# Window attention and a highway layer on one core: the steps of five engines laid out in one order table

## The chip, the cores and the metric

The kernel runs on one core of a Trainium2 chip. The core has a matrix engine (TensorE, PE in the profile, with its weight loads as PEld), VectorE (DVE), ScalarE (ACT), GpSimd (POOL) and a queue for transfers (SyncE, SP), each with its own queue of instructions. The metric is the device time of the core in microseconds (us), from the launch's first to its last instruction; lower is better.

## The reference

Attention over 4 batches, 8 heads, 768 positions of 64 elements. A query sees the first 4 positions (the sink) and the 128 positions up to its own (the window). The result, as 3072 tokens of 512 elements, goes through a highway layer.

```python
keep = is_sink | ((rel >= 0) & (rel < 128))      # rel = query position - key position
a = softmax(where(keep, q @ k.T / 8, -1e9))
x = (a @ v).reshape(3072, 512)
H = maximum(x @ w_h, 0)
T = 1 / (1 + exp(-(x @ w_t + b_t)))
out = T * H + (1 - T) * x
```

## The kernel before

The work is cut into NB = 24 blocks of 128 queries, 6 per batch. Keys and values of block n are a chunk of 128 rows shifted by 64, so a block's queries need their own chunk whole ("A" parts, 128 columns of EW = 192) and half of the chunk on either side ("B" parts, 64 columns). Block n therefore needs q of n and k and v of n-1, n and n+1.

A block goes through these steps. pe_T (L222) transposes q or k by head pairs on TensorE into the second half of a score tile's PSUM banks, and act_T (L232) copies the transpose out to SBUF as qT or kT, on ScalarE, or on VectorE where an engine is given. pe_SA and pe_SB (L266, L275) make the scores, four heads in each of two groups g; act_S (L288) takes the exponential of one group on ScalarE, into e; dve_mask (L295) multiplies it by the window's mask on VectorE. pe_sink (L249) makes the sink scores of one block, or of two blocks at a time after the first batch, and act_sink (L258) their exponential, es. pe_AB and pe_AA (L304, L317) sum the values, with a column of 2.0 beside each head's values that gives the softmax's denominator. dve_rec and dve_x (L334, L339) divide: x, in the program xh. pe_X (L346) transposes x, act_X (L353) copies the transpose to SBUF as xT. pe_Mt and pe_Mh (L358, L372) multiply by w_t (after a bias row) and by w_h; act_u (L367) takes a tanh of the first; dve_d, dve_e and dve_o (L380, L386, L392) form max(h, 0) - x, times (1 + u), plus 2x, and the output's transfer starts. The factors of 2 take the place of the sigmoid, and undo each other.

Order is written by hand. Under manual_schedule every engine runs its instructions in the order in which the program calls the steps, so a wait of one instruction holds all that its engine has behind it. Semaphores for the data between engines are added for it.

PSUM is what couples the steps. The pool ps_s has two score tiles, one per group; a transpose of q or k lies in such a tile as well, either in a tile that a block's scores use next (it is then "hosted" by that block), or in a tile of its own ("lone"). A tile is free again when the exponential and the copy have read it. The pool ps_m has two banks, which sink scores, xtp, tps and hps take in turn in the order of the program: the third of them waits until the first has been read. ps_av holds the values of one block.

Loads run ahead by AHEAD = 8 blocks, all issued by GpSimd, one instruction for each of q, k and v. In the start GpSimd issues q0, k0, k1, v0, v1, q1 and k2, then makes the four triangles of the mask, then goes on with w_h and later loads. VectorE's more_constants (L184) clears buffers, waits for the mask, makes two variants of it (mask0, mask1) and scales the bias (bt16).

Blocks 0 to 3 are written out one call after another: the scores of a block come group by group (lone_S, scores and exponential of group 0 and then of group 1), and transposes are lone, q on ScalarE and k on VectorE. From block 3 on a loop over i runs the steps of several blocks: the scores of n = i + 1, the masks of group 1 of i, xT of i - 1 on VectorE, d and e of i - 2, the values of i, the sink scores of n, o of i - 2, the gate and h of i - 1, the transpose of x of i. So h is one block behind the values, and d, e and o two. From n = TS = 5 on block n hosts the transposes of q and k of n + 2.

Of the kernel before, what the change touches and what calls it, by code (L numbers as in the profile page):

```python
# [20 lines left out]
def kernel(  # L21
# [106 lines left out]
    with tc.manual_schedule(engines={ENG.DVE}):  # L128
        nc.vector.memset(k_first[0:HP], 0.0)
        nc.vector.memset(v_ring[0][0:HP, 0:H * 65], 0.0)  # L130
        nc.vector.memset(warm, 0.0)
        nc.vector.memset(ident, 1.0)
        nc.vector.memset(ebias, _EXP_BIAS)
        nc.vector.memset(mask, 1.0)
        nc.vector.memset(bm, 1.0)
        for vt in v_ring:
            init_v(vt)

    def tri(t, rows, lo, hi, base, step, cm):
        nc.gpsimd.affine_select(  # L140
# [11 lines left out]
    with tc.manual_schedule(engines={ENG.Pool, ENG.SP}):  # L152
        nc.sync.dma_start(out=bt32, in_=moe_b_t.unsqueeze(0))
        for b in range(B):
            nc.sync.dma_start(out=vs_dn[b], in_=v[b, :, 0:NSINK, :])
        load_q(0)
        load_k(0)
        load_k(1)
        nc.gpsimd.affine_select(
            out=ident, in_=ident, compare_op=ALU.is_equal, fill=0.0,  # L160
            base=0, pattern=[[-1, P]], channel_multiplier=1)
        load_v(0)
        load_v(1)
        load_q(1)
        load_k(2)
        tri(mask, slice(0, HP), 0, P, HP - 1, -1, 1)
        tri(mask, slice(HP, P), 0, P, 0, 1, -1)
        tri(mask, slice(0, HP), P, EW, 0, 1, -1)
        tri(mask, slice(HP, P), P, EW, -1, -1, 1)
        load_w(moe_w_h, wh_sb)  # L170
        nc.gpsimd.affine_select(
            out=bm, in_=bm, compare_op=ALU.is_ge, fill=0.0,
            base=0, pattern=[[-NSINK, H]], channel_multiplier=1)
        nc.gpsimd.affine_select(
            out=bm, in_=bm, compare_op=ALU.is_ge, fill=0.0,
            base=NSINK - 1, pattern=[[NSINK, H]], channel_multiplier=-1)
        load_v(2)
        load_q(2)
        load_k(3)
        load_w(moe_w_t, wt_sb)  # L180
        load_v(3)


    def more_constants():  # L184
        nc.vector.memset(bt16, 0.0)
        nc.vector.memset(ones_row, 0.0)
        nc.vector.memset(ones_row[0:1, :], 1.0)
        for i in range(2):
            nc.vector.memset(ks_bd[i], 0.0)
            nc.vector.memset(vs_bd[i], 0.0)  # L190
            nc.vector.memset(es_t[i], 0.0)
        nc.vector.tensor_copy(out=mask0, in_=mask)
        nc.vector.memset(mask0[0:HP, 0:P], 0.0)
        nc.vector.memset(mask0[HP:HP + NSINK, 0:P], 1.0)
        nc.vector.memset(mask0[HP:P, P:EW], 0.0)
        nc.vector.tensor_copy(out=mask1, in_=mask)
        nc.vector.memset(mask1[HP:HP + NSINK, P:EW], 0.0)
        nc.vector.tensor_scalar_mul(bt16[0:1, :], bt32, 0.5)

    def sink_ones():  # L200
        for i in range(2):
            nc.vector.tensor_scalar_mul(vs_bd[i][0:NS4, :, D:D + 1],
                                        bm[0:NS4, :].unsqueeze(2), 2.0)
# [110 lines left out]
                    rhs=vt[src, 65 * h:65 * h + _AVN], start=(h % 4 == 0), stop=False,  # L314
                    skip_group_check=True)

    def pe_AA(n):  # L317
        av = av_of[n]
        vt = v_ring[n % NV]
        b, c = divmod(n, NSC)  # L320
        for h in range(H):
            nc.tensor.matmul(  # L322
                av[:, h // 4, h % 4, 0:_AVN], lhsT=e_at(n, h)[:, 0:P],
                rhs=vt[:, 65 * h:65 * h + _AVN], start=False,
                stop=False, skip_group_check=True)
        if c:
            for g in range(2):
                nc.tensor.matmul(
                    av[:, g, :, 0:65], lhsT=es_of[n],
                    rhs=vs_bd[b % 2][:, 4 * g:4 * g + 4, :], start=False, stop=True,  # L330
                    skip_group_check=True)
        av_of[n] = av.rearrange("p g h e -> p (g h) e")
# [65 lines left out]
    def on(n):  # L398
        return 0 <= n < NB

    def has_sink(n):
        return 0 < n < NSC or on(n) and n % 2 == 1

    def load_set(n):
        if on(n):
            load_q(n)
            load_k(n + 1)
            load_v(n + 1)

    def lone_T(nq, nk):  # L410
        if nq is not None:
            pe_T(("q", nq), 0, q_sd.pop(nq))
            act_T(("q", nq), 0, qT, nq)
        if nk is not None:
            pe_T(("k", nk), 1, k_sd.pop(nk))
            act_T(("k", nk), 1, kT, nk, nc.vector.tensor_copy)

    def lone_S(n):
        for g in range(2):
            pe_SA(n, g)  # L420
            pe_SB(n, g)
            act_S(n, g)

    TS = 5

    with tc.manual_schedule(engines={ENG.PE, ENG.DVE, ENG.Activation, ENG.SP, ENG.Pool}):
        warm_up(8)
        more_constants()
        for n in range(3, AHEAD):
            load_set(n)  # L430
        pe_T("q0", 0, q_sd.pop(0))
        act_T("q0", 0, qT, 0)
        pe_T("k0", 1, k_sd.pop(0))
        act_T("k0", 1, kT, 0, nc.vector.tensor_copy)
        pe_T("k1", 0, k_sd.pop(1))
        act_T("k1", 0, kT, 1)
        lone_S(0)
        dve_mask(0, 0)
        dve_mask(0, 1)
        lone_T(1, 2)  # L440
        sink_ones()
        sink_v(0, nc.vector)
        fill_ks(0, nc.vector)
        pe_AB(0)
        pe_AA(0)
        dve_rec(0)
        dve_x(0)
        lone_S(1)
        pe_sink(1)
        act_sink(1)  # L450
        dve_mask(1, 0)
        dve_mask(1, 1)
        pe_X(0)
        act_X(0)
        pe_AB(1)
        pe_AA(1)
        dve_rec(1)
        dve_x(1)
        pe_Mh(0)
        dve_d(0)  # L460
        pe_X(1)
        act_X(1)
        pe_Mh(1)
        dve_d(1)
        lone_T(2, 3)
        lone_S(2)
        pe_Mt(0)
        act_u(0)
        dve_mask(2, 0)
        dve_mask(2, 1)  # L470
        dve_e(0)
        dve_o(0)
        pe_Mt(1)
        act_u(1)
        pe_sink(2)
        act_sink(2)
        dve_e(1)
        dve_o(1)
        pe_AB(2)
        pe_AA(2)  # L480
        dve_rec(2)
        dve_x(2)
        lone_T(3, 4)
        pe_X(2)
        act_X(2)
        lone_S(3)
        pe_sink(3)
        act_sink(3)
        dve_mask(3, 0)
        dve_mask(3, 1)  # L490
        lone_T(4, 5)
        for n in range(AHEAD, AHEAD + 3):
            load_set(n)
        for i in range(3, NB + 2):
            n = i + 1
            load_set(i + AHEAD)
            if i == TS - 1:
                lone_T(n + 1, None)
            hosts = n >= TS
            if on(n):  # L500
                for g in range(2):
                    if hosts and on(n + 2):
                        pe_T(n, g, (q_sd, k_sd)[g].pop(n + 2))
                    elif hosts and g and n + 2 == NB:
                        pe_T(n, g, k_sd.pop(n + 2))
                    pe_SA(n, g)
                for g in range(2):
                    pe_SB(n, g)
                act_S(n, 0)
                if hosts and on(n + 2):  # L510
                    act_T(n, 0, qT, n + 2)
            if on(i):
                dve_mask(i, 1) if i > 3 else None
                if i > 3:
                    act_X(i - 1, nc.vector.tensor_copy)
            elif on(i - 1):
                act_X(i - 1, nc.vector.tensor_copy)
            if 0 <= i - 2 and i > 3:
                dve_d(i - 2)
                dve_e(i - 2)  # L520
            if on(i):
                pe_AB(i)
                pe_AA(i)
                dve_rec(i)
                dve_x(i)
            if has_sink(n):
                pe_sink(n)
                act_sink(n)
            if i > 3:
                dve_o(i - 2)  # L530
            if on(n):
                dve_mask(n, 0)
                act_S(n, 1)
            if on(i - 1):
                pe_Mt(i - 1)
                act_u(i - 1)
                pe_Mh(i - 1)
            if on(n) and hosts and n + 2 <= NB:
                act_T(n, 1, kT, n + 2)
            if on(i):  # L540
                pe_X(i)
            if i + 2 < TS + 1:
                lone_T(i + 2, i + 3)
            if n % NSC == NSC - 1 and on(n + 1):
                b = (n + 1) // NSC
                fill_ks(b, nc.gpsimd)
                sink_v(b, nc.gpsimd)


# [33 lines left out]
```

The softmax here doesn't subtract the row's maximum and nothing guards it: scores larger than these inputs give would overflow.

## Time and profile before

| | |
|---|---|
| time, median of 3 runs | 134.98 us (133.96 to 139.13) |
| the profiled run | 134.23 us, span 132.5 us, mean granted TensorE clock 0.965 |
| busy: PE, DVE, ACT, POOL | 112.5, 106.4, 81.7, 76.4 us |
| exponentials e, ScalarE, 48 | 896 ns each |
| copies of q and k, ScalarE, 43; VectorE, 6 | 577 ns; 416 ns |
| copies of xT, VectorE, 21; ScalarE, 3 | 418 ns; 576 ns |
| tanh u, ScalarE, 24 | 589 ns |
| masks on e, VectorE, 48 | 570 ns |
| d, e, x, o on VectorE, 24 each | 682, 703, 692, 684 ns |
| loads of q, k, v, from issue to landing | 6.2 to 6.5 us (median) |
| the chain that ended last | DVE 48%, PE 32%, ACT 7%, POOL 6% |

The span runs from the first to the last instruction. Busy time counts an engine's instructions, with overlaps counted once; matmuls are pipelined, so their single times (386 ns for 512 columns) are longer than the pace at which they follow each other. The row of slices cuts the span in 40 equal parts, each digit a busy share in tenths; the clock row has the share of full TensorE clock that was granted. The chain of waits goes back from the last instruction, at each step to what released it. A timeline line gives start, length, engine, line and operation, and in brackets the idle time before it and what ended that.

### The profile page before, as it was taken

What the parts mean: (1) busy time and instruction counts of PE and PEld (TensorE: products, weight loads), DVE (VectorE), ACT (ScalarE), POOL (GpSimd) and SP (SyncE); (2) the same over time, 40 slices, a digit from 0 to 9 for tenths busy, and PEclk for the clock granted to TensorE, in tenths of its full rate; (3) what the DMA queues carried; (4) which work ended last, traced back from release to release, by engine and by line L of the source; (5) the groups of instructions that cost most, each with busy time, mean ns of one, the idle gap of its engine ahead of it and who ended that gap; (6) DMA issues with size and microseconds to landing.
All of it is one profiled execution on the core that took longest, in us unless ns stands there. A gap on an engine that the chain in (4) does not pass through costs nothing.

```text
span 132.5 us, 4673 instructions
## 1 busy us (share of the span) xinstructions
PE 112.5 (85%) x1984; PEld 70.2 (53%) x1984; DVE 106.4 (80%) x249; ACT 81.7 (62%) x133; POOL 76.4 (58%) x102
## 2 busy tenths in 40 slices
PE   4715987867996999998998999999999999998830
PEld 1203653444745556675566566766667656665410
DVE  7624934594338999999899999999999999999990
ACT  3115341746456789777877698777977779762110
POOL 6999995779979879999779999301200000000000
PEclk9999999996579999999999999999999999999996
DMA  0999999999999999999999999992022210222122
GB/s 5 116 118 133 160 172 156 154 129 218 167 156 152 150 152 142 173 151 201 199 200 174 117 193 191 161 218 84 9 84 84 79 53 31 79 84 80 70 88 79
DMA packets 79701, 17.10 MB, mean 129 GB/s; under 512 B 75585, under 2 KB 76609, under 8 KB 79682
## 3 DMA queue, kind: packets, MB, share of 16 engines
q0 software_dynamic: 76064, 10.49, 122.4%
q1 hardware_dynamic: 3618, 6.33, 13.5%
q8 instruction: 15, 0.25, 0.8%
q14 instruction: 4, 0.03, 0.1%
HBM read 21.01 MB, written 6.29 MB: 206 GB/s over the span
## 4 chain that ended last, share of the span: by engine, by line
DVE 48%; PE 32%; ACT 7%; POOL 6%; issue 4%; DVEq 0%; POOLq 0%; ACTq 0%
DVE e L298 11%; DVE ee L388 9%; DVE otok L394 8%; DVE xh L341 8%; PE hps L376 7%; DVE dd L382 6%; PE tps L363 6%; ACT e L290 4%; DVE xT L355 4%; PE av L322 3%; PE av L312 3%; PE sps L229 2%; PE sps L272 2%; PE sps L285 2%; PE xtp L350 2%
## 5 line engine op out<-in xcount | busy, mean ns | idle before, releaser
L290 ACT ACTIVATE e<-sps,ebias 128x768 f16<-128x768 f32 x48 | 42.5, 896 | 21.3 <-PE sps L285 21.3
L298 DVE TENSOR_TENSOR e<-e,mask 128x768 f16<-128x768 f16 x48 | 25.8, 570 | 5.5 <-ACT e L290 5.5
L234 ACT COPY t<-sps 128x512 f16<-128x512 f16 x43 | 24.8, 577 | 8.0 <-PE sps L229 8.0
L104 POOL DMA_DIRECT2D v<-in_v_dram x28 | 23.9, 854 | 4.8 <-DMA ksd<-in_k_dram 1.4
L376 PE MATMUL hps<-wh_sb,xT 128*128 128x512 f16 x96 | 25.4, 388 | 0.7 <-ACT xT L355 0.7
L363 PE MATMUL tps<-wt_sb,xT 128*128 128x512 f16 x96 | 25.2, 386 | 0.0
L90 POOL DMA_DIRECT2D qsd<-in_q_dram x24 | 22.2, 923 | 2.9 <-DMA wt_sb<-in_moe_w_t_dram 1.2
L97 POOL DMA_DIRECT2D ksd<-in_k_dram x27 | 23.3, 869 | 0.5 <-issue 0.2
L369 ACT ACTIVATE u<-tps 128x512 f16<-128x512 f32 x24 | 14.1, 589 | 8.1 <-PE tps L363 8.1
L388 DVE SCALAR_TENSOR_TENSOR ee<-u,dd 128x512 f16<-128x512 f16 x24 | 16.9, 703 | 2.3
L382 DVE SCALAR_TENSOR_TENSOR dd<-hps,xh 128x512 f16<-128x512 f32 x24 | 16.4, 682 | 1.9 <-PE hps L376 1.9
L341 DVE TENSOR_TENSOR xh<-av,rec 128x512 f16<-128x512 f32 x24 | 16.6, 692 | 0.8
L272 PE MATMUL sps<-t,t 64*128 64x128 f16 x192 | 13.1, 229 | 4.2 <-DVE t L234 3.3
L394 DVE SCALAR_TENSOR_TENSOR otok<-xh,ee 128x512 f32<-128x512 f16 x24 | 16.4, 684 | 0.1
L376 PEld LDWEIGHTS <-xT 128*128 128x128 f16 x96 | 9.5, 100 | 12.2 <-ACT xT L355 0.8
L312 PE MATMUL av<-v,e 64*64 64x66 f16 x384 | 13.2, 199 | 2.3 <-DVE e L298 1.4
L363 PEld LDWEIGHTS <-xT 128*128 128x128 f16 x96 | 9.6, 100 | 9.9 <-issue 1.5
L312 PEld LDWEIGHTS <-e 64*64 64x64 f16 x384 | 9.8, 113 | 4.1 <-DVE e L298 2.6
L350 PEld LDWEIGHTS <-xh 128*128 128x128 f16 x96 | 7.3, 99 | 8.1 <-issue 2.7
L322 PE MATMUL av<-v,e 128*128 128x66 f16 x192 | 11.1, 201 | 0.2 <-issue 0.2
L350 PE MATMUL xtp<-ident,xh 128*128 128x128 f16 x96 | 9.5, 222 | 1.6 <-DVE xh L341 1.6
L361 PE MATMUL tps<-bt,ones_row 128*128 128x512 f16 x24 | 9.4, 390 | 0.5 <-DVE xT L355 0.5
(61 smaller groups left out, 128.5 us busy)
## 6 DMA issues: line engine op xcount, KB each, us to landing
out_dram<-otok SPq DMA_DIRECT2D x24, 256.0 KB, 4.5
qsd<-in_q_dram POOLq DMA_DIRECT2D x24, 128.0 KB, 6.3
ksd<-in_k_dram POOLq DMA_DIRECT2D x20, 128.0 KB, 6.2
v<-in_v_dram POOLq DMA_DIRECT2D x20, 128.0 KB, 6.5
v<-in_v_dram POOLq DMA_DIRECT2D x8, 64.0 KB, 6.5
wh_sb<-in_moe_w_h_dram POOLq DMA_DIRECT2D x1, 512.0 KB, 6.4
wt_sb<-in_moe_w_t_dram POOLq DMA_DIRECT2D x1, 512.0 KB, 7.9
ksd<-in_k_dram POOLq DMA_DIRECT2D x7, 64.0 KB, 7.1
```

Source lines behind the costliest of these rows:

```text
L97: nc.gpsimd.dma_start(out=ksd[rows], in_=k[b, :, s0:s0 + nr, :].transpose([1, 0, 2]))
L104: nc.gpsimd.dma_start(out=vt[rows, :, 0:D], in_=v[b, :, s0:s0 + nr, :].transpose([1, 0, 2]))
L234: (eng or nc.scalar.copy)(out=t.rearrange("p a (h b) -> p h a b", b=HP), in_=t_view(s_tile(n, g)))
L290: nc.scalar.activation(out=e.rearrange("p a b c -> p a (b c)"), in_=s_tile(n, g)[:, :, 0:2 * EW], func=AF.Exp, bias=ebias, scale=SCALE)
L298: nc.vector.tensor_tensor(out=ev, in0=ev, in1=m.unsqueeze(1).to_broadcast([P, 4, EW]), op=ALU.mult)
L312: nc.tensor.matmul(av[part, h // 4, h % 4, 0:_AVN], lhsT=e_at(n, h)[src, P:EW], rhs=vt[src, 65 * h:65 * h + _AVN], start=(h % 4 == 0), sto ...
L341: nc.vector.tensor_tensor(out=xh.rearrange("p (h d) -> p h d", d=D), in0=av_of.pop(n)[:, :, 0:D], in1=rec_of.pop(n).unsqueeze(2).to_broadc ...
L363: nc.tensor.matmul(tps, lhsT=xT[:, kc, :], rhs=wt_sb[:, kc, :], start=False, stop=(kc == NOC - 1))
L376: nc.tensor.matmul(hps, lhsT=xT[:, kc, :], rhs=wh_sb[:, kc, :], start=(kc == 0), stop=(kc == NOC - 1))
L382: nc.vector.scalar_tensor_tensor(out=dd, in0=h_of.pop(n), scalar=0.0, in1=xh_of[n], op0=ALU.max, op1=ALU.subtract)
L388: nc.vector.scalar_tensor_tensor(out=ee, in0=u_of.pop(n), scalar=1.0, in1=dd_of.pop(n), op0=ALU.add, op1=ALU.mult)
L394: nc.vector.scalar_tensor_tensor(out=otok, in0=xh_of.pop(n), scalar=2.0, in1=ee_of.pop(n), op0=ALU.mult, op1=ALU.add)
```

## The change

The written-out first blocks and the loop are replaced by one table, ORDER, of 450 steps, each a name and a block number, run one after another. Each engine's order is the order of its steps in the table. What each step computes is as before.

What differs in the order: xT is copied on ScalarE in 16 blocks ("xT") and on VectorE in 8 ("xTV"), where it was 3 and 21; lone copies of q and k are on ScalarE except for k5 and q7 ("tkV", "tqV"). In most odd blocks the sink scores ("sk") stand ahead of the values ("A"). The highway's h ("Mh") is two blocks behind the values, and the gate ("Mt") one. The masks of both groups and d, e, o stand in other places among VectorE's steps. The first blocks are interleaved: both groups' scores are one step ("S"), and the first gate and h multiplications stand between later blocks' scores and values. Hosting starts at block 4: blocks 4 and 5 host q of n + 1, later ones q of n + 2; k of n + 2 throughout.

In the start, GpSimd makes the mask's triangles before it issues q1, v1 and k2, clears of buffers move to the first group of VectorE's instructions, and the scaling of the bias moves behind the first masks. The aim is to keep TensorE and VectorE from waiting for each other, and to have the first blocks reach the full pace sooner.

```diff
@@ first VectorE instructions
         for vt in v_ring:
             init_v(vt)
+        nc.vector.memset(bt16, 0.0)
+        nc.vector.memset(ones_row, 0.0)
...
@@ GpSimd's first instructions
         load_v(0)
-        load_v(1)
-        load_q(1)
-        load_k(2)
         tri(mask, slice(0, HP), 0, P, HP - 1, -1, 1)
...
         tri(mask, slice(HP, P), P, EW, -1, -1, 1)
+        load_q(1)
+        load_v(1)
+        load_k(2)
         load_w(moe_w_h, wh_sb)
...
-    def more_constants():
-        nc.vector.memset(bt16, 0.0)
...
+    def more_masks():
         nc.vector.tensor_copy(out=mask0, in_=mask)
...
+    def sink_ones():
         nc.vector.tensor_scalar_mul(bt16[0:1, :], bt32, 0.5)
-    def sink_ones():
...
+    TS = 6
+    H0 = 4
+    def hosted(n, g):
+        if n < H0:
+            return None
+        m = n + 2 if g or n >= TS else n + 1
+        return m if m < NB + g else None
...
+    def pe_S(n):
+        for g in range(2):
+            if hosted(n, g) is not None:
+                pe_T(n, g, (q_sd, k_sd)[g].pop(hosted(n, g)))
+            pe_SA(n, g)
+        for g in range(2):
+            pe_SB(n, g)
...
+    def do_A(n):
+        pe_A(n)
+        load_set(n + AHEAD)
...
+    ORDER = """
+    Tq:0 Tk:0 tq:0 tk:0 Tk:1 tk:1 S:0 x0_:0 x1_:0 m0_:0 m1_:0 fk:0 Tk:2 Tq:1 tk:2 A:0 tq:1 xh:0
+    S:1 sk:1 x0_:1 X:0 xTV:0 x1_:1 m0_:1 es:1 m1_:1 A:1 Tq:2 xh:1 Tk:3 tq:2 tk:3 X:1 xT:1 S:2
+    sk:2 x0_:2 Mh:1 es:2 m0_:2 x1_:2 Mh:0 d:1 m1_:2 d:0 A:2 Tq:3 xh:2 Tk:4 tq:3 tk:4 S:3 X:2
+    x0_:3 Mt:1 xTV:2 x1_:3 m0_:3 sk:3 Tk:5 u:1 m1_:3 Tq:4 es:3 tkV:5 Mt:0 tq:4 e:1 sk:4 o:1 u:0
+    S:4 es:4 e:0 A:3 x0_:4 o:0 Mh:2 x1_:4 xh:3 Mt:2 tq:5 d:2 tk:6 m0_:4 sk:5 u:2 S:5 m1_:4 es:5
+    e:2 X:3 x0_:5 A:4 xTV:3 o:2 x1_:5 Mt:3 xh:4 tq:6 tk:7 m0_:5 Tq:7 u:3 X:4 tqV:7 S:6 xT:4
+    m1_:5 A:5 x0_:6 Mh:3 x1_:6 xh:5 Mt:4 tq:8 d:3 tk:8 m0_:6 S:7 u:4 m1_:6 e:3 sk:7 x0_:7 X:5
...
+    x0_:10 Mh:7 x1_:10 xh:9 Mt:8 tq:12 d:7 tk:12 m0_:10 X:9 u:8 m1_:10 S:11 xT:9 e:7 sk:11
+    x0_:11 o:7 A:10 es:11 m0_:11 x1_:11 Mh:8 xh:10 tq:13 Mt:9 d:8 tk:13 m1_:11 X:10 u:9 S:12
+    xTV:10 e:8 A:11 x0_:12 o:8 Mh:9 x1_:12 xh:11 Mt:10 tq:14 d:9 tk:14 m0_:12 X:11 u:10 m1_:12
...
+    x0_:22 Mt:20 tk:24 d:19 m0_:22 X:21 u:20 m1_:22 S:23 xT:21 e:19 A:22 x0_:23 o:19 sk:23 Mt:21
+    es:23 xh:22 x1_:23 m0_:23 Mh:20 u:21 m1_:23 X:22 d:20 A:23 xT:22 e:20 Mh:22 xh:23 Mh:21 d:22
+    d:21 X:23 xT:23 o:20 Mt:22 e:21 Mh:23 o:21 u:22 e:22 Mt:23 d:23 o:22 u:23 e:23 o:23
+    """
...
-        for i in range(3, NB + 2):
...
+        for step in ORDER.split():
+            op, n = step.split(":")
+            STEP[op](int(n))
```

In the table T, t, S, x0_/x1_, m0_/m1_, sk, es, A, xh, X, xT, Mh, Mt, u, d, e, o are the steps above: pe_T, act_T, the scores, the two groups' exponentials and masks, sink scores and their exponential, the values, the division, and the highway's steps. "fk" fills the first sink keys and values and scales the bias, on VectorE.

More of the change, by code (lines that the diff above doesn't have):

```diff
@@ L137 @@
             init_v(vt)
+        nc.vector.memset(bt16, 0.0)
+        nc.vector.memset(ones_row, 0.0)
+        nc.vector.memset(ones_row[0:1, :], 1.0)
+        for i in range(2):
+            nc.vector.memset(ks_bd[i], 0.0)
+            nc.vector.memset(vs_bd[i], 0.0)
+            nc.vector.memset(es_t[i], 0.0)
     def tri(t, rows, lo, hi, base, step, cm):
@@ L181 @@
         load_v(3)
-    def more_constants():
-        nc.vector.memset(bt16, 0.0)
[L186 to L191, printed above, removed]
+    def more_masks():
         nc.vector.tensor_copy(out=mask0, in_=mask)
@@ L315, in pe_AB, with pe_A @@
                     skip_group_check=True)
-    def pe_AA(n):
+    def pe_A(n):
+        pe_AB(n)
         av = av_of[n]
@@ L402, in has_sink, with copy_T @@
         return 0 < n < NSC or on(n) and n % 2 == 1
+    TS = 6
[5 more added lines that the diff above has]
+        return m if m < NB + g else None
+    host_of = {}
+    for n in range(NB):
+        for g in range(2):
+            if hosted(n, g) is not None:
+                host_of[hosted(n, g), g] = n
+    def pe_S(n):
+        for g in range(2):
+            if hosted(n, g) is not None:
+                pe_T(n, g, (q_sd, k_sd)[g].pop(hosted(n, g)))
+            pe_SA(n, g)
+        for g in range(2):
+            pe_SB(n, g)
+    def copy_T(m, g, eng=None):
+        act_T(host_of.get((m, g), ("t", m, g)), g, (qT, kT)[g], m, eng)
+        if g and m and m % NSC == 0 and m < NB:
+            fill_ks(m // NSC, nc.gpsimd)
+            sink_v(m // NSC, nc.gpsimd)
     def load_set(n):
@@ L408, in load_set, with first_sinks @@
             load_v(n + 1)
[L410 to L424, printed above, removed]
+    def first_sinks(_):
+        fill_ks(0, nc.vector)
+        sink_ones()
+        sink_v(0, nc.vector)
@@ new lines, in do_A, with norm @@
+    def do_A(n):
+        pe_A(n)
+        load_set(n + AHEAD)
+    def norm(n):
+        dve_rec(n)
+        dve_x(n)
+    STEP = {
+        "Tq": lambda n: pe_T(("t", n, 0), 0, q_sd.pop(n)), "tq": lambda n: copy_T(n, 0),
+        "Tk": lambda n: pe_T(("t", n, 1), 1, k_sd.pop(n)), "tk": lambda n: copy_T(n, 1),
+        "tqV": lambda n: copy_T(n, 0, nc.vector.tensor_copy),
+        "tkV": lambda n: copy_T(n, 1, nc.vector.tensor_copy),
+        "S": pe_S, "x0_": lambda n: act_S(n, 0), "x1_": lambda n: act_S(n, 1),
+        "m0_": lambda n: dve_mask(n, 0), "m1_": lambda n: dve_mask(n, 1),
+        "sk": pe_sink, "es": act_sink, "A": do_A, "xh": norm,
+        "X": pe_X, "xT": act_X, "xTV": lambda n: act_X(n, nc.vector.tensor_copy),
+        "Mh": pe_Mh, "Mt": pe_Mt, "u": act_u, "d": dve_d, "e": dve_e, "o": dve_o,
+        "fk": first_sinks,
+    }
@@ new lines @@
+    m1_:5 A:5 x0_:6 Mh:3 x1_:6 xh:5 Mt:4 tq:8 d:3 tk:8 m0_:6 S:7 u:4 m1_:6 e:3 sk:7 x0_:7 X:5
+    o:3 A:6 es:7 xTV:5 x1_:7 Mh:4 xh:6 tq:9 Mt:5 d:4 tk:9 m0_:7 X:6 u:5 m1_:7 S:8 xT:6 e:4 A:7
+    x0_:8 o:4 Mh:5 x1_:8 xh:7 Mt:6 tq:10 d:5 tk:10 m0_:8 X:7 u:6 m1_:8 S:9 xT:7 e:5 A:8 x0_:9
+    o:5 sk:9 x1_:9 xh:8 Mh:6 es:9 m0_:9 tq:11 Mt:7 d:6 tk:11 m1_:9 X:8 e:6 u:7 S:10 xT:8 o:6 A:9
+    x0_:10 Mh:7 x1_:10 xh:9 Mt:8 tq:12 d:7 tk:12 m0_:10 X:9 u:8 m1_:10 S:11 xT:9 e:7 sk:11
+    x0_:11 o:7 A:10 es:11 m0_:11 x1_:11 Mh:8 xh:10 tq:13 Mt:9 d:8 tk:13 m1_:11 X:10 u:9 S:12
@@ new lines @@
+    xTV:10 e:8 A:11 x0_:12 o:8 Mh:9 x1_:12 xh:11 Mt:10 tq:14 d:9 tk:14 m0_:12 X:11 u:10 m1_:12
+    S:13 xT:11 e:9 sk:13 x0_:13 o:9 A:12 es:13 m0_:13 Mh:10 x1_:13 xh:12 Mt:11 tq:15 d:10 tk:15
+    m1_:13 X:12 u:11 S:14 xTV:12 e:10 A:13 x0_:14 o:10 Mh:11 x1_:14 xh:13 Mt:12 tq:16 d:11 tk:16
+    m0_:14 X:13 u:12 m1_:14 S:15 xT:13 e:11 sk:15 x0_:15 o:11 A:14 es:15 m0_:15 x1_:15 Mh:12
+    xh:14 tq:17 Mt:13 d:12 tk:17 m1_:15 X:14 u:13 e:12 S:16 xT:14 o:12 A:15 x0_:16 Mh:13 x1_:16
+    xh:15 Mt:14 tq:18 d:13 tk:18 m0_:16 X:15 u:14 m1_:16 S:17 xT:15 e:13 sk:17 x0_:17 o:13 A:16
@@ new lines @@
+    es:17 m0_:17 x1_:17 Mh:14 xh:16 tq:19 Mt:15 d:14 tk:19 m1_:17 X:16 u:15 S:18 xTV:16 e:14
+    A:17 x0_:18 o:14 Mh:15 x1_:18 xh:17 Mt:16 tq:20 d:15 tk:20 m0_:18 X:17 u:16 m1_:18 S:19
+    xT:17 e:15 sk:19 x0_:19 o:15 A:18 es:19 m0_:19 Mh:16 x1_:19 xh:18 Mt:17 tq:21 d:16 tk:21
+    m1_:19 X:18 u:17 S:20 xTV:18 e:16 A:19 x0_:20 o:16 Mh:17 x1_:20 xh:19 Mt:18 tq:22 d:17 tk:22
+    m0_:20 X:19 u:18 m1_:20 S:21 xT:19 e:17 A:20 x0_:21 o:17 sk:21 x1_:21 xh:20 Mh:18 es:21
+    m0_:21 tq:23 Mt:19 d:18 tk:23 m1_:21 X:20 u:19 e:18 S:22 xT:20 A:21 o:18 x1_:22 Mh:19 xh:21
@@ L426 @@
+    x0_:22 Mt:20 tk:24 d:19 m0_:22 X:21 u:20 m1_:22 S:23 xT:21 e:19 A:22 x0_:23 o:19 sk:23 Mt:21
+    es:23 xh:22 x1_:23 m0_:23 Mh:20 u:21 m1_:23 X:22 d:20 A:23 xT:22 e:20 Mh:22 xh:23 Mh:21 d:22
+    d:21 X:23 xT:23 o:20 Mt:22 e:21 Mh:23 o:21 u:22 e:22 Mt:23 d:23 o:22 u:23 e:23 o:23
+    """
     with tc.manual_schedule(engines={ENG.PE, ENG.DVE, ENG.Activation, ENG.SP, ENG.Pool}):
         warm_up(8)
-        more_constants()
+        more_masks()
         for n in range(3, AHEAD):
             load_set(n)
-        pe_T("q0", 0, q_sd.pop(0))
@@ L432 @@
[L432 to L493, printed above, removed]
-        for i in range(3, NB + 2):
[L495 to L547, printed above, removed]
```

## The prediction

> **What bounds it now.** I read the page first: busy time by engine and the rows of slices.
>
> ```profile
> PE 112.5 (85%) x1984; PEld 70.2 (53%) x1984; DVE 106.4 (80%) x249; ACT 81.7 (62%) x133; POOL 76.4 (58%) x102
> ...
> PE   4715987867996999998998999999999999998830
> ...
> DVE  7624934594338999999899999999999999999990
> ACT  3115341746456789777877698777977779762110
> ...
> PEclk9999999996579999999999999999999999999996
> ```
>
> A slice is 3.3 us. Two regions show: a ramp of 13 slices in which no engine is full and in which the TensorE clock falls to about 0.6 in slices 10 to 12, and a middle in which PE and DVE are both full. So I asked the view of stages for four single blocks of the middle and for the bad stretch of the ramp.
>
> ```profile
> 30.00:40.00 10.00, 8.76 (x131) 5.53 (x132) 3.61 (x9) 5.76 (x10) 9.00 (x12) 0.66 2.20 180
> ...
> 45.86:49.76 3.90, 3.90 (x87) 2.48 (x91) 3.76 (x8) 3.14 (x5) 3.20 (x5) 1.00 2.12 159
> ...
> 57.89:62.19 4.30, 4.30 (x95) 2.92 (x99) 4.16 (x10) 3.54 (x6) 4.30 (x6) 1.00 2.22 194
> ...
> 100.67:104.78 4.11, 4.11 (x85) 2.71 (x84) 3.97 (x9) 3.52 (x6) 0.00 (x0) 1.00 0.19 69
> ```
>
> Columns: stretch, length, then busy time of PE, PEld, DVE, ACT, POOL, the granted clock, DMA. Up to 62 us the period is 3.90 us for a block without sink scores and 4.30 with them, PE busy all through: a mean of 4.10. From 65 us on each block takes 4.11 whichever it is. The chain of waits in order of time says why:
>
> ```profile
> 100.67 0.33 DVE xT L355
> 101.00 0.61 DVE dd L382
> 101.70 0.69 DVE ee L388
> 102.55 0.69 DVE xh L341
> 103.24 0.60 DVE otok L394
> 103.84 0.94 DVE e L298 x2
> 104.78 0.34 DVE xT L355
> ```
>
> VectorE carries the chain without a gap, 4.11 us a block. PE's work is as long (4.10), so **taking work from VectorE alone cannot shorten the steady block**; it can only remove slips. From the values of block 5 (45.94 us in the timeline) to those of block 23 (121.27) are 75.3 us for 18 blocks, against 18 x 4.10 = 73.8, less 0.7 for three blocks (6, 12, 18) without sink values (0.23 each): 73.1. About 2.2 us are slips. The rest of the loss is the ramp: the values of block 5 begin at 45.94, where five blocks of 4.1 after the first landing at 5.3 would be some 26.
>
> **What the Trainium skill says.** "TensorE: Matmul & The Clock Gate", Part 1 on the HAM clock gate: the array's clock is halved after an idle window of some 3.4 us and comes back after a busy one. The trace agrees: PE has 1.58 us without work before 30.37, and the clock is 0.66 in 30:40; four 128x512 matmuls that take 0.86 us warm take 1.39 there. "PSUM — Partial Sum Buffer", Engine vs sequencer instructions: the queues of ScalarE and VectorE are strict FIFO and matmuls start in program order, so an order table is the schedule. "ScalarE: Activation LUTs", What ACT_TABLE_LOAD costs: instructions back to back overlap by about 93 ns; two exponentials of 896 ns take 1.69 us here, an overlap of 0.10. "SBUF — State Buffer", Who interferes with whom: a VectorE instruction with two SBUF inputs contends with a GpSimd one that reads SBUF. Two masks take 1.86 us at 69.73, beside GpSimd's sink values, against 1.02 elsewhere.
>
> **Part by part. Copies.** xT leaves VectorE in 13 more blocks (21 copies there before, 8 after), and 4 more q/k copies (6 before, 2 after): VectorE loses 13 x 0.418 + 4 x 0.416 = 7.1 us busy, ScalarE gains 13 x 0.576 + 4 x 0.577 = 9.8. With the overlap, ScalarE's block is 2 x 0.80 for the exponentials, 2 x 0.48 for q and k, 0.49 for tanh, 0.18 for the mean sink: 3.23, with xT 3.71. VectorE's is 4.11 - 0.34 = 3.77 with xT gone. Both are below PE's 4.10, so the added ScalarE work lies beside matmuls: nothing on the path.
>
> **Middle order.** Per block PE now runs S, (sk), A, Mh of two before, Mt of one before, X. It is the same matmuls. Walked through from the end of S:11 at t=0: sk to 0.45, A:10 to 1.34, Mh:8 to 2.24, Mt:9 to 3.32, X:10 to 3.6, S:12 to 4.3. ScalarE: x0 at 0.16, es 0.96, x1 1.32, q and k copies to 3.1, so S:12's banks are free in time. VectorE: mask 1.06, xh 1.6 to 2.5, d:8 to 3.15 (it frees the bank that X:10 wants at 3.3: 0.15 to spare), second mask to 3.6, ahead of A:11 at 4.3. The waits of the new order thus close; what queues behind d:8, should it be late, is X:10 and all of PE. The slips: three GpSimd collisions, up to 0.84 each today, at most 0.3 on PE once VectorE has slack, and a fetch gap like the 0.63 at 62.5: I allow 1.4 of today's 2.2.
>
> **Ramp.** GpSimd makes the masks before the loads of q1, v1, k2, so they are ready at about 6.3 and VectorE's mask work (1.04) ends near 7.4 instead of 9.9; it no longer stands before the copy of k0 (10.29 today, after which PE starts at 10.75):
>
> ```profile
> 10.29 0.40 DVE L234 COPY t<-sps 128x512 f16<-128x512 f16 x1
> ...
> 10.75 0.40 PE L272 MATMUL sps<-t,t 64*128 64x128 f16 x4 [3.32 <-DVE t L234]
> ...
> 30.37 0.40 PE L350 MATMUL xtp<-ident,xh 128*128 128x128 f16 x4 [1.58 <-DVE xh L341]
> ```
>
> All three first copies are on ScalarE, done at 8.05; the first exponential starts at 8.7 instead of 11.45. But v1 and k2 are issued at 7.25 and 8.15, and early loads take 4.1 to 4.9 us to land (bounds on both: 11.4 and 13.1; I take 12.2). k2's transpose stands ahead of A:0 on PE, so A:0 starts near 12.8 (13.52 today), S:1 at 14.2 (14.92), A:1 ends at 19.0 (19.6). The bias scaling and sink values hide before xh:0. Then the order pays: the transposes of block 2 follow A:1 at once, S:2 ends near 21.7 (24.9), Mh:1 and Mh:0, still half cold, end at 24.9, A:2 runs 25.25 to 26.2 (27.28 to 28.45), S:3 near 27.7 (30.70), and S:4, with Mt:1, Mt:0 and two sinks ahead of it, ends near 32.8. From there PE is full: A .88, Mh .90, Mt 1.08, sk .22, S .71, X .32, A .88, Mt 1.08, the lone transpose .12, X .32, S .71 and 0.8 of waits: A:5 starts at 40.8 instead of 45.94, 5.1 earlier. No cold stretch is in this sum.
>
> **Tail.** After A:23 come two Mh that today lie partly before it. PE is as long; then tanh 0.6, e and o, with VectorE some 0.5 behind: 2.6 after the last matmul (2.25 today), and 3.2 from the last o to the end of the span, as now.
>
> **Sum.** PE's work from A:5 on, by pieces of warm blocks: 19 A x 0.88, 17 S x 0.71, 20 Mt x 1.08, 21 Mh x 0.90, 19 X x 0.32, sinks 3.8, less 0.7: 78.5. 40.8 + 78.5 + 1.4 + 2.6 + 3.2 = 126.5 span. The median today lies 2.5 above the span (134.98 against 132.5): **129.0 us**.
>
> **Rivals.** (1) The clock falls back in the new ramp. For: after A:2 PE idles about 1.2 us until both copies are done, and today a window with 1.58 idle sufficed. Against: the rest of the window is full. Mt:1, Mt:0 and S:4 then run at half rate, some 4.6 us of PE work doubled, less the idle time in it: +2.2, 131.2. (2) ScalarE binds the middle. For: by busy times alone its block is 4.34 with xT and 4.15 in the mean, and tanh, xT and the next exponential stand in one queue. Against: the overlap above, and 3.71. At 4.25 a block it costs 18 x 0.15 = 2.7: 131.7. (3) The longer lag and two-bank rotation starve PE: d late, X late, S late. For: the 0.15 us to spare. Against: VectorE then has 0.3 us of slack a block. 0.45 lost in 18 blocks costs 8.1: 137.1, slower than before. It also holds if v1 and k2 land very late.
>
> **Chances.** Forecast 0.52, rival 1 0.25, rival 2 0.15, rival 3 0.08. The range goes down to 125.8 (loads at 11.4, slips of 0.2 in place of 1.4, last VectorE lag gone: 0.8 + 1.2 + 0.5, and 0.7 for a median nearer the span) and up to 132.6, past rivals 1 and 2. Within 2% (132.3 to 137.7) fall the worst of rivals 1 and 2 and most of rival 3.
>
> **What would show it.** First exponential near 8.7; A:5 near 40.8; PEclk without a dip after slice 8 (rival 1 has one); a middle whose blocks alternate 3.90 and 4.30 with PE carrying the chain, VectorE at about 99 us busy and ScalarE at 91; no PE idle behind dd L382 (rival 3) and none behind ScalarE's copies (rival 2). A:1 later than 20 us, or a middle block over 4.2, would prove the walk wrong.

## The result, and the profile after

The new kernel takes 130.77 us (median of 4, 130.1 to 132.41), the kernel before 134.63 us beside it; ratio 0.971, interval 0.963 to 0.980. Run a second time, beside the last experiments, the ratio was 0.963 (0.955 to 0.971). The forecast was 129.0, range 125.8 to 132.6: right side, inside the range, 1.8 us too low. Some executions of a kernel come out slower than its others, whatever the kernel (139.13 us of the kernel before), and ratios, their intervals in brackets, and means leave those out. Each ratio is to the kernel before, run beside it on the same chip.

The new kernel's page, busy time and slices:

```profile
span 128.8 us, 4699 instructions
...
PE 109.5 (85%) x1984; PEld 68.6 (53%) x1984; DVE 102.3 (79%) x232; ACT 90.7 (70%) x150; POOL 76.4 (59%) x102
...
PE   4841948979999769997999999999899999999830
...
DVE  7618432548996939994999999989999999899990
ACT  3253626448989857999688879989689798893310
...
PEclk9999999999999999999999999999999999999997
```

The ramp is shorter: PE is full from slice 10 on (29 us) instead of 14 (43 us). Then come two holes, in slices 14 and 15 (42 to 48 us, PE 7 and 6) and in slice 19 (58 to 61 us, PE 7); the middle of the kernel before has no digit under 8. In the second hole PE stands for 0.81 us at 59.15, in the middle of block 9's values, and waits for nothing that the profile shows; the kernel before has such a gap, of 0.63 us, at the same place in its work. To measure ramp, middle and tail, I cut each span where the values of block 5 and those of block 23 begin on PE. The view of stages of the new kernel, columns as before:

```profile
0.00:40.56 40.56, 30.25 (x520) 18.43 (x522) 25.23 (x90) 23.11 (x38) 34.01 (x49) 1.00 1.72 134
40.56:116.76 76.20, 72.91 (x1428) 47.03 (x1420) 68.54 (x129) 65.27 (x109) 42.41 (x53) 1.00 1.36 139
116.76:128.80 12.04, 6.37 (x54) 3.11 (x52) 8.53 (x14) 2.37 (x4) 0.00 (x0) 0.94 0.23 87
```

and of the kernel before:

```profile
45.94:121.27 75.33, 73.33 (x1430) 47.57 (x1422) 72.28 (x144) 58.67 (x96) 36.80 (x46) 1.00 1.18 127
121.27:132.50 11.23, 5.30 (x47) 2.72 (x47) 7.46 (x13) 1.19 (x2) 0.00 (x0) 0.89 0.24 89
```

The ramp is 5.4 us shorter (40.56 against 45.94). The middle is 0.9 longer (76.20 against 75.33) although VectorE works 3.7 us less in it, and the tail 0.8 longer. 5.4 - 0.9 - 0.8 = 3.7, the difference of the spans (132.5 - 128.8). Where nothing slips, the chain of waits is PE's alone:

```profile
101.60 0.25 PE sps L285 x16
101.85 0.26 PE av L312 x16
102.11 0.37 PE av L323 x8
102.48 0.23 PE av L329 x2
102.70 0.86 PE hps L377 x4
103.78 0.86 PE tps L364 x4
105.43 0.25 PE sps L285 x16
```

That is 3.83 us for a block without sink scores. Blocks with them take some 4.3. That is the pace of PE's work, a little under the 3.90 and 4.30 that it had in the kernel before up to 62 us. From 65 us on VectorE held the kernel before at 4.11 for every block, and there the new order is faster: from the division of block 16 to that of block 22 the new kernel takes 23.62 us, the kernel before 24.65, 0.17 more a block. Over the whole middle the slips hide this.

**The slip at block 6.** Timeline, 44 to 47 us:

```profile
44.87 0.68 POOL L104 DMA_DIRECT2D v<-in_v_dram  x1 [0.28 <-DVE ee L389]
45.54 0.46 POOL L243 COPY ks<-t 64x16 f16<-64x16 f16 x2
46.06 0.62 PE L254 MATMUL sk<-t,ks 128*128 128x128 f16 x8 [1.72 <-POOL ks L243]
```

GpSimd fills the sink keys (L243) of batch 1 out of k6, whose copy is done at 35.8 us. But the fill stands in GpSimd's queue behind the load sets of blocks 10 and 11, and these go out until 45.5. The sink scores of block 7 wait 1.72 us for it, and behind them on PE the values of block 6. From the division of block 5 to that of block 6 are 6.21 us; without the wait they are 4.27 (fill_ahead, below).

### The profile page after: what moved, and what is told of

Same layout as the page of the kernel before. It is cut to its first block, busy times and chain, and to the rows that moved or that the text cites. A ratio compares the mean times of both kernels' runs of the same rounds, so it can differ in the third digit from the quotient of the medians.

```text
span 128.8 us, 4699 instructions
## 1 busy us (share of the span) xinstructions
PE 109.5 (85%) x1984; PEld 68.6 (53%) x1984; DVE 102.3 (79%) x232; ACT 90.7 (70%) x150; POOL 76.4 (59%) x102
## 4 chain that ended last, share of the span: by engine, by line
PE 66%; DVE 10%; POOL 8%; DMA 6%; ACT 4%; issue 4%; POOLq 0%; ACTq 0%
PE hps L377 14%; PE tps L364 13%; PE av L323 6%; DMA v<-in_v_dram 6%; PE av L312 6%; PE xtp L351 5%; PE sps L229 4%; PE sps L272 4%; PE sps L285 4%; PE sk L254 4%; PE tps L362 4%; PE av L329 3%; DVE dd L383 3%; DVE xh L342 2%; POOL v L104 2%
## 5 line engine op out<-in xcount | busy, mean ns | idle before, releaser
L290 ACT ACTIVATE e<-sps,ebias 128x768 f16<-128x768 f32 x48 | 41.3, 895 | 5.9 <-PE sps L285 5.8
L364 PE MATMUL tps<-wt_sb,xT 128*128 128x512 f16 x96 | 24.6, 379 | 0.0
L312 PE MATMUL av<-v,e 64*64 64x66 f16 x384 | 11.2, 197 | 2.9 <-DMA v<-in_v_dram 2.1
L272 PE MATMUL sps<-t,t 64*128 64x128 f16 x192 | 12.6, 227 | 1.2 <-ACT t L234 1.2
L356 ACT COPY xT<-xtp 128x512 f16<-128x512 f16 x16 | 9.3, 583 | 3.3 <-PE xtp L351 3.2
L312 PEld LDWEIGHTS <-e 64*64 64x64 f16 x384 | 8.7, 111 | 4.6 <-DVE e L298 2.3
L337 DVE RECIPROCAL rec<-av 128x8 f32<-128x8 f32 x24 | 4.9, 205 | 7.8 <-PE av L329 6.5
L229 PE MATMUL sps<-ident,ksd 64*128 64x64 f16 x192 | 7.1, 196 | 4.5 <-DMA ksd<-in_k_dram 4.5
```

The source lines that it names most:

```text
L272: nc.tensor.matmul(sps[:, hh, hl * EW:hl * EW + P], lhsT=kT[n][rows, hp, :], rhs=qT[n][rows, hp, :], start=True, stop=True)
L290: nc.scalar.activation(out=e.rearrange("p a b c -> p a (b c)"), in_=s_tile(n, g)[:, :, 0:2 * EW], func=AF.Exp, bias=ebias, scale=SCALE)
L312: nc.tensor.matmul(av[part, h // 4, h % 4, 0:_AVN], lhsT=e_at(n, h)[src, P:EW], rhs=vt[src, 65 * h:65 * h + _AVN], start=(h % 4 == 0), sto ...
L364: nc.tensor.matmul(tps, lhsT=xT[:, kc, :], rhs=wt_sb[:, kc, :], start=False, stop=(kc == NOC - 1))
```

## The experiments

Theory A at first: the first blocks bring the gain, the new middle none. Theory B: the middle's order and ScalarE's copies bring it. Two kernels split the program where the scores of block 4 begin.

**ramp_only: new first blocks, old loop.**

```diff
-    ... S:4 es:4 e:0 A:3 x0_:4 o:0 Mh:2 ...   (all from S:4 on)
+    e:0 o:0
+        for i in range(3, NB + 2):            (the loop of the kernel before)
```

> New start and new order up to the scores of block 4, then the old loop from block 3's values on. Theory A (the first blocks bring the gain, the new middle brings none): the scores of block 4 start near 32.3 us as in the new kernel instead of 33.7, the clock does not fall after them, blocks then take 4.1 us as before; 129.5 to 131.5 us in all, about as fast as the new kernel. Theory B (the new middle order and the copies on ScalarE bring the gain): 133 to 135 us.

Measured 133.23 us, ratio 0.984 (0.973 to 0.995): less than theory A asked. Its timeline and its clock row show why:

```profile
48.59 0.87 POOL L104 DMA_DIRECT2D v<-in_v_dram  x1 [0.82 <-DMA v<-in_v_dram]
49.46 0.47 POOL L243 COPY ks<-t 64x16 f16<-64x16 f16 x2
49.98 1.03 PE L254 MATMUL sk<-t,ks 128*128 128x128 f16 x8 [2.90 <-POOL ks L243]
```

```profile
PEclk9975555699999995999999999999999999999998
```

The division of block 5 comes at 43.52 us (47.07 before), 3.55 early. Then comes the same wait, 2.90 us here, and behind it the clock falls: the row has a 5 in slice 16 (49.6 to 52.9 us), and the eight matmuls of the sink scores take 1.03 us, which took 0.62 in the new kernel. Block 7 takes 8.19 us in all, and its division is at 55.82, where the kernel before has 55.29.

**rest_only: old first blocks, new order from the scores of block 4 on** (the mirror image of the edit above, with the sink scores of block 4 called in between).

> Old start and old order up to the scores of block 4, then the new order. Theory A: the clock falls as before near 31 us, only blocks 4 and 5 gain from the new order (1 to 2 us), the middle and tail lose 0.9 and 0.8: 133.5 to 135.5 us. Theory B: 131 to 132 us.

Measured 134.31 us, ratio 0.985 (0.974 to 0.996). The time lies where theory A put it, but the ratio shows some gain, as large as that of the other half. By the ratios neither half gives the whole, though the intervals all but touch those of the new kernel; the product of the two, 0.984 x 0.985 = 0.969, is near what it has. Theory A in its plain form falls, because ramp_only is not about as fast as the new kernel, and so does B, because rest_only is not. The trace of ramp_only shows that the first blocks gain more than comes through.

**xt_vector: x's transposes back on VectorE.**

```diff
-    xT:4 ... xT:6 ... xT:22
+    xTV:4 ... xTV:6 ... xTV:22      (14 blocks)
```

> New kernel with x's transpose copied on VectorE in all of blocks 4 to 22 (14 more than in the new kernel, 14 x 0.42 us of VectorE). If VectorE's slack is what holds PE at its pace, VectorE carries the chain again at 4.11 us a block and its collisions with GpSimd fall on the path: 1 to 2.5 us slower, 132 to 133. If PE's own work and order set the middle, VectorE (90% busy there) takes it in: within 0.5 us of the new kernel.

Measured 131.36 us, ratio 0.971 (0.963 to 0.978), not told from the new kernel's 0.971 and 0.963. The trace shows a small loss: from the division of block 16 to that of block 22 are 24.05 us, not 23.62, and from 111 us on VectorE is in the chain again. That is 0.07 us a block, too little for the times to show. For the most part PE's work sets the middle.

**old_start: GpSimd's start as before.**

```diff
         load_v(0)
+        load_v(1)
+        load_q(1)
+        load_k(2)
         tri(mask, slice(0, HP), 0, P, HP - 1, -1, 1)
...
-        load_q(1)
-        load_v(1)
-        load_k(2)
```

> New kernel with GpSimd's old order at the start: v1, q1, k2 issued before the mask's triangles. As predicted (masks early are worth it): first masks on e wait for the mask until about 9.9 us, no later than the first exponential ends, but k2 lands 1.4 us earlier, so values of block 0 start near 11.8 instead of 12.8. If the landing of v2 (17.85 us, issued at 10.36) bounds block 1's values anyway, the end moves by less than 0.5 us; if the reordering of GpSimd's start is needed, 1 us slower or more.

Measured 130.87 us, ratio 0.966 (0.956 to 0.975): no loss. The first mask runs at 9.97 us (9.93 in the new kernel) and the values of block 0 at 11.39 instead of 12.83; then those of block 1 wait 2.58 us for v2. The early masks are worth nothing here, since the first one on e has to wait for its exponential until then anyway, and the loads behind them come later for it.

Theory C, from ramp_only: the early ramp runs into GpSimd's fill, whose time is set by the loads ahead of it. Theory D: keys and queries themselves are late there. Four kernels for it, which ran together on one chip. The new kernel did not run there, and the kernel before was slower there (136.31 us, against 135.41 and 134.99 beside the other experiments), so a ratio of these four set against one of the new kernel is weaker evidence than one set against another of the four.

**fill_vector: fills on VectorE.**

```diff
-            fill_ks(m // NSC, nc.gpsimd)
-            sink_v(m // NSC, nc.gpsimd)
+        "F": lambda b: (fill_ks(b, nc.vector), sink_v(b, nc.vector)),   (behind o:2, o:8, o:14)
```

> New kernel with the sink keys and values of batches 1 to 3 filled by VectorE (after o of blocks 2, 8, 14) instead of GpSimd. Theory C (the ramp's gain is eaten at block 7: GpSimd's fill stands behind loads that go at the transfers' pace, and sink scores of block 7 wait for it 1.7 us): that wait and the slow VectorE instructions beside GpSimd's fills (1.32 and 1.21 us) go, VectorE gets 3 x 1.4 us of work: 1.5 to 2.5 us faster than the new kernel, 128 to 129.3. Theory D (loads of keys and queries themselves are late there, or VectorE has no room): no faster than 130.3.

Measured 130.35 us, ratio 0.957 (0.954 to 0.960). The wait goes: 4.27 us from block 5 to block 6, not 6.21. But VectorE's fill takes part of it back, 5.58 us instead of 4.20 from the division of block 3 to that of block 4. A gain, smaller than expected; its interval overlaps that of the new kernel's second run.

**fill_ahead: two load sets behind the fill.**

```diff
             sink_v(m // NSC, nc.gpsimd)
+            for late in ((10, 11) if m == NSC else ()):
+                load_set(late)
...
-        load_set(n + AHEAD)
+        load_set(n + AHEAD) if n not in (2, 3) else None
```

> New kernel with the load sets of blocks 10 and 11 called after GpSimd's fill for batch 1 instead of before it; nothing else. Theory C: the wait of the sink scores of block 7 goes, the collisions of GpSimd with VectorE stay: 1 to 2 us faster than the new kernel, 128.7 to 129.8. Theory D: same as the new kernel, or slower as the loads come later.

Measured 129.06 us, ratio 0.948 (0.945 to 0.952), below both intervals of the new kernel. Its timeline:

```profile
38.02 0.68 POOL L243 COPY ks<-t 64x16 f16<-64x16 f16 x2
...
44.66 1.43 POOL L104 DMA_DIRECT2D v<-in_v_dram  x2
44.80 0.45 PEld L254 LDWEIGHTS <-ks 128*128 128x128 f16 x8
44.81 0.62 PE L254 MATMUL sk<-t,ks 128*128 128x128 f16 x8
```

```profile
42.16 0.21 DVE L337 RECIPROCAL rec<-av 128x8 f32<-128x8 f32 x1 [1.13 <-PE av L329]
...
116.20 0.20 DVE L337 RECIPROCAL rec<-av 128x8 f32<-128x8 f32 x1
```

The fill runs at 38.02 instead of 45.54, the sink scores start without a wait, and block 6 takes 4.27 us. The loads called later do no harm that shows. From the division of block 5 to that of block 23 (the two lines above) are 74.04 us, where the new kernel has 76.35 and the kernel before 75.79: with the wait gone the new middle is shorter than the old one. This is what theory C says, and D falls.

**v2_early: v2 ahead of w_h.**

```diff
+        load_v(2)
         load_w(moe_w_h, wh_sb)
...
-        load_v(2)
```

> New kernel with the load of v2 issued ahead of that of w_h. Values of block 1 then no longer wait 2.07 us for v2. Theory C: blocks 1 to 6 come 1 to 1.5 us sooner, and the sink scores of block 7 wait that much longer for GpSimd's fill, which the transfers time: within 0.5 us of the new kernel. If the ramp's waits simply add: 1 to 1.5 us faster.

Measured 131.65 us, ratio 0.965 (0.961 to 0.970). The division of block 1 comes at 18.94 instead of 19.67, that of block 5 at 41.28 instead of 41.63; then the sink scores wait 2.2 us, and block 6 takes 7.55 instead of 6.21:

```profile
46.20 1.03 PE L254 MATMUL sk<-t,ks 128*128 128x128 f16 x8 [2.20 <-POOL ks L243]
```

The fill runs at 45.7 us, as in the new kernel (45.5), though the blocks ahead of it are earlier. What is won ahead of the fill is lost at it, as theory C says, and more than that, because the clock falls behind the longer wait: 1.03 us for the eight matmuls, not 0.62.

**fill_vector_v2: both.**

> Both edits: fills on VectorE and v2 ahead of w_h. Theory C: now the earlier ramp comes through, 1 to 1.5 us faster than with the fills on VectorE alone: 127 to 128.3 us. If something else at the loads' pace bounds blocks 7 to 10, no faster than the fills on VectorE alone.

Measured 129.33 us, ratio 0.950 (0.946 to 0.953): 0.7% under fill_vector on the same chip, where v2 alone brought nothing that shows (0.965). With the fill out of the way the ramp's gain comes through, though a little less than expected. The pair v2_early and fill_vector_v2 is the cleanest test of theory C by time: one chip, and only the engine of the fills differs, 0.965 (0.961 to 0.970) against 0.950 (0.946 to 0.953).

**after_again, sink_behind, h_one_behind and fill_ahead_v2** ran together on one chip, the first being the new kernel as their base.

> The new kernel itself, on the chip of the next three runs, as their base: a ratio of 0.965 to 0.975 to the kernel before, with the sink scores of block 7 waiting 1.5 to 2.5 us for GpSimd's fill.

Measured 129.78 us, ratio 0.963, just under what was expected; the sink scores waited 2.0 us.

> New kernel with the sink scores of blocks 7, 11, 13, 15, 17 and 19 (and their exponential) moved behind the values, nothing else. If the place of the sink scores matters for ScalarE's order, odd blocks lose 0.2 to 0.5 us each, 1 to 3 us in all; if PE's work sets the block, within 0.5 us of the new kernel.

```diff
-    sk:13 x0_:13 o:9 A:12 es:13
+    x0_:13 o:9 A:12 sk:13 es:13        (and so in five other odd blocks)
```

Measured 130.52 us, ratio 0.961 (0.951 to 0.972): no difference that shows, though an interval this wide would hide 1 us. The loss of up to 3 us that the place of the sink scores could have meant did not come.

> New kernel with h of blocks 4 to 20 one block behind the values, right after the gate, as before, with d ahead of e of the block before it and the sink scores behind the values (so that no bank waits for d). The matmuls are the same. If only PE's work sets the middle: within 0.7 us of the run with the sink scores behind the values. If the lag of two is what lets PE run on, 0.2 us or more a block: 3 us or more slower.

```diff
-    S:14 xTV:12 e:10 A:13 ... Mh:11 xh:13 Mt:12 tq:16 d:11 tk:16
+    S:14 xTV:12 d:11 e:10 A:13 ... xh:13 Mt:12 Mh:12 tq:16 tk:16
```

Measured 138.53 us, ratio 1.029 (1.021 to 1.036): slower than the kernel before, and by the means (138.4 and 129.3 us) 9 us slower than sink_behind, with the same matmuls. Timeline of its middle:

```profile
96.43 1.03 ACT L234 COPY t<-sps 128x512 f16<-128x512 f16 x2
...
97.38 0.58 ACT L370 ACTIVATE u<-tps 128x512 f16<-128x512 f32 x1
...
98.01 0.38 PE L351 MATMUL xtp<-ident,xh 128*128 128x128 f16 x4 [0.72 <-ACT u L370]
...
99.25 1.69 ACT L290 ACTIVATE e<-sps,ebias 128x768 f16<-128x768 f32 x2 [1.30 <-PE sps L285]
```

Two banks go round. With the order gate, h, x's transpose, the transpose takes the gate's bank and so waits for the tanh, which stands behind two exponentials and two copies on ScalarE. The transpose in its turn holds back the next scores, and these the next exponential: ScalarE now has 28% of the chain of waits (4% in the new kernel), and most blocks take 4.4 to 5.1 us. With h two behind and ahead of the gate, the transpose takes h's bank, which VectorE's d has freed. In the kernel before, whose h was one behind, ScalarE had the tanh ahead of k's copy and no x to copy. So I read the lag as belonging with the new ScalarE order; the old lag with the old ScalarE order inside the new table was not run.

> New kernel with the load sets of blocks 10 and 11 called after GpSimd's fill for batch 1, and v2 loaded ahead of w_h. Theory C: with the wait for the fill gone the 0.7 us that v2 brings in the first blocks come through: 2.2 to 3.0 us faster than the new kernel, a ratio near 0.945 to the kernel before. If the fill's or the loads' pace still bounds block 7, no more than 1.8 us faster.

Measured 128.06 us (median of 6), the lowest of all; ratio 0.953 (0.947 to 0.959) against the 0.963 of after_again. By the means (128.2 and 129.5 us) it is 1.3 us under after_again, less than theory C asked. The chain of waits of its profile shows where v2's gain stayed:

```profile
12.12 7.27 DMA ksd<-in_k_dram
...
19.44 0.40 PE sps L229 x8
...
21.82 3.41 PE hps L377 x8
```

Now k3, issued at 12.12, lands only at 19.39 and holds block 2's transposes, and both h multiplications run at half pace. The division of block 1 comes 1.24 us earlier than in after_again (18.13 for 19.37), that of block 2 no longer does (26.50 for 26.44). Whether v2 early adds anything to fill_ahead, run on another chip, is not settled.

## Why the prediction was right, and where not

**Bound.** Right in the main: PE's work sets the block, and taking 14 copies back to VectorE left the time as it was. But VectorE's 4.11 was not quite PE's pace. Six blocks of the late middle take 23.62 us, 3.94 each, so the steady block did get shorter, which the prediction had ruled out for work taken from VectorE alone; of the 1.03 us over these six blocks, xt_vector gives 0.43 to the copies.

**Ramp.** Right in size at its end: block 5 at 40.56 for 40.8. The first exponential came at 8.99 for 8.7, but block 1 gained nothing from it:

```profile
19.63 0.21 DVE L336 RECIPROCAL rec<-av 128x8 f32<-128x8 f32 x1 [1.74 <-PE av L328]
```

```profile
16.29 1.01 DVE L298 TENSOR_TENSOR e<-e,mask 128x768 f16<-128x768 f16 x2
...
17.98 0.65 PE L312 MATMUL av<-v,e 64*64 64x66 f16 x16 [2.07 <-DMA v<-in_v_dram]
...
19.67 0.21 DVE L337 RECIPROCAL rec<-av 128x8 f32<-128x8 f32 x1 [2.36 <-PE av L329]
```

The first line is the division of block 1 in the kernel before, the others are from the new kernel. The masks on e are done at 17.30, and from there the walk's 19.0 for the end of block 1's values would have come true. But v2, a load that the walk left out, lands at 17.85, and they end at 19.63. So the earlier start, which was credited to the early mask, is lost at v2, and old_start shows that the mask brings none of it.

All of the ramp's gain comes behind block 1. By their divisions the new kernel is 2.65 us ahead at block 2, 2.10 at block 3, 4.60 at block 4 and 5.44 at block 5. The 2.50 between blocks 3 and 4 (6.70 us before, 4.20 now) lie where the clock of the kernel before had fallen. How much of the gain is the clock and how much the interleaved order was not run apart.

The prediction read that fall as agreeing with the idle window of some 3.4 us that the Trainium skill gives ("TensorE: Matmul & The Clock Gate", Part 1). The trace shows the halving but no such window: from 27.7 to 31.1 us, just ahead of the fall, PE was busy for 1.82 of 3.4 us.

**Middle.** The step that failed is the 1.4 us allowed for slips. From block 5 to block 23 the walk had 72.4 of PE's work (its 78.5 less 6.1 from block 23's values on) and 1.4 of slips, 73.8; measured 76.20. The term missing is GpSimd's queue, which was counted for its three collisions alone, while the fill stands there behind loads. An earlier ramp makes that worse, since the fill does not come sooner. It costs about 2 us (6.21 against 4.27), most of the 2.4 missing, and without it, in fill_ahead, the middle takes 74.04 us, near the walk's 73.8. GpSimd's collisions were priced at 0.3 and cost some 0.65 each for batches 2 and 3: block intervals of 4.35 us (3.71 for the same block in v2_early) and 5.05 (4.40 in fill_vector).

**Middle order.** The walk's bank order was right, and h_one_behind shows what it is worth: rival 3's mechanism, a transpose that waits for a bank, is real, but the change's order is the one that avoids it. Rival 2 did not come: ScalarE has 4% of the chain. Rival 1 did not come behind block 2's values, where PE idled 0.56 and 0.20 us for the copies, not 1.2. Its mechanism came elsewhere, behind the longer waits for the fill in ramp_only and v2_early.

**Tail and busy times.** 8.9 us from block 23's values to the end of the last o, for 8.7. ScalarE 90.7 busy for 91; VectorE 102.3 for 99. Busy time counts overlaps once, and VectorE's instructions overlap by some 0.08 us where they run back to back (before, o starts at 103.16 us and the division ahead of it ends at 103.24). A copy that goes takes two such overlaps with it where a gap stays in its place: by estimate 17 x 2 x 0.08 = 2.7 us of the 7.1. Subtracting means times counts was wrong there.

**Sum.** The span came out at 128.8 for 126.5, 2.3 too low, and nearly all of it is the middle. The median is only 1.8 off because it lies 2.0 above the span of the profiled run, where the prediction added 2.5; that part is luck.

## What to carry to other kernels

When a stage is made earlier, ask what is tied to a clock of its own, here the loads on GpSimd's queue, and which compute instruction stands behind them: the gain is lost at the first such meeting. Calling two sets of loads behind that instruction (fill_ahead) took some 2 us out of the middle. Judge an order by which bank each matmul inherits and which engine's queue frees it, not by the lag itself. And when work is taken from one of two engines that are almost equally full, the other sets the pace, and little is gained.

## What was not expected of the hardware

The clock row of the new kernel reads 9 all through the ramp, while the eight matmuls of h in blocks 1 and 0 take 2.86 us; eight of these take 1.74 in the tail. First the new kernel's chain of waits, twice, then the clock row of fill_ahead:

```profile
22.71 2.86 PE hps L377 x8
...
117.81 1.74 PE hps L377 x8
```

```profile
PEclk9985555599999999999999999999999999999996
```

In fill_ahead the eight take 3.40 us, and its row says so. The row of the new kernel does not, nor that of the kernel before, in which four of them take 1.55 us at 19.59 and 0.86 at 44.15: parts of the first 24 us ran at about half pace in all three. The mean clock of a run is no guide either: executions of the new kernel with means of 0.994, 0.930 and 0.918 took 130.48, 130.10 and 131.07 us. The spacing of 512-column matmuls tells the pace, 0.43 us each in fill_ahead and 0.22 in the tail (3.40 and 1.74 for eight).

A wait can cost more than its length. Behind the wait for the fill of 1.72 us (2.0 in after_again) the clock stayed full; behind 2.20 us in v2_early and 2.90 in ramp_only it was at half for a slice, and block 6 or 7 paid for both. Where the limit lies was not measured.
